# Features by relu and an exponential in place in PSUM, output low parts on GpSimd, P's low part in two halves

## The chip, the cores and the metric

The kernel runs on one core of one Trainium2 chip. The metric is device time in microseconds (us) of one execution. The core has five engines, each with its own instruction queue, in order: TensorE (PE, matmuls; PEld are its weight loads), VectorE (DVE), ScalarE (ACT), GpSimd (POOL) and SyncE (SP, which issues the DMAs here). SBUF is the working memory, PSUM the memory that matmuls write. In this kernel POOL works on SBUF only; DVE and ACT also read PSUM.

## The reference

Two layers, each of an attention with a compressive memory and of a gated MLP, with residuals:

```
x = x + A(layernorm(x)); x = x + B(layernorm(x))        # twice, S = 2048, D = 640

A: q, k, v = x@wq, x@wk, x@wv in 32 heads of 20, 4 segments of 512 rows; M = z = 0
   for each segment s:
       p    = softmax(qs ks^T / sqrt(20) + causal mask)
       phi(t) = t + 1 if t > 0 else exp(t)
       a_mem = (phi(qs) M) / (phi(qs) z + 1e-6)
       o    = g * a_mem + (1 - g) * (p vs)               # g = sigmoid(beta), by head
       M, z = M + phi(ks)^T vs, z + sum(phi(ks))
   return concat(o) @ wo
B: z = gelu(x@w_in); z1, z2 = halves; (w_sp @ layernorm(z2) + b_sp) * z1 @ w_out
```

All of it is in float32. The kernel gets there with float16 matmuls: a float32 value is split into a high part (its float16 rounding) and a low part (what is left, in float16), and a product takes three matmuls, high x high, high x low, low x high. Making a low part takes one operation that subtracts the high part from the value.

phi can be written without a branch as max(t, 0) + min(exp(t), 1). Both kernels use that form.

## The kernel before, in words

Each layer is three stages: attention (`phase1a`, class `Attention`), the output projection with the first MLP matmul (`phase1b`), and the spatial matmul with the last one (`phase2`). The change is in the attention, and in a few constants that the prologue makes.

**Attention by slots.** 64 pairs of heads (16 in each of 4 segments) are worked off at three slots each, 192 slots a layer; `run` (L912) writes their order out by hand. In slot t, for pair n = t // 3:

- `scores` (L793): PE forms a third of the transposed scores of pair n (tile `es`, one PSUM buffer) and a third of the untransposed scores of pair n + 2 (tile `mp`, one buffer), with the masks (L818, L790). ACT turns `es` into P by an exponential (L827). DVE takes row maxima of `mp` (L834) into `mx`; at a pair's last third it splits them into `mhs` (L838, L839, eight elements a row each).
- `pvs` (L865): PE multiplies P's high and low parts (PH, PL) with the values (L877), head h of pair n - 1 or so, three slots after they are made.
- `maxes` (L853): PE transposes `mhs` (`mtp`, L858), ACT copies it (L860), two DMAs on SP (L863) write it into two rows of the pair's q tile in `qk`, so that the scores come with their maxima subtracted.
- `cast` (L841): ACT rounds a head's P to float16 (PH, L849), POOL subtracts (PL, L850; 128 x 1280). PH and PL have two buffers each. For the last TAIL = 4 pairs of a layer, head 1's subtraction goes to DVE.
- `combine` (L881): DVE scales PV's sums (L888 to L893), POOL adds the halves and the memory's part (L894, L896) into `ot`; when a unit's heads are complete, `out` is posted two slots later: high part on ACT (L904), low part on DVE (L905), two DMAs on SP into `o_d` (L908).

**Dense work in between.** The rest of each slot on PE is filled with pieces of the next projections, by times planned in `run` (`plan`, `timed`, `until`): `value` (v of a row tile), `project` (wo for finished rows) and `unit` (L653), which forms q and then k of 128 of the 640 columns, each as 15 matmuls (L668) into a PSUM tile of tag "dn" (two buffers, shared by q, k, v and the projection). When such a tile is complete, `out` (L675) posts what follows for the next slots:

- one slot later `parts`: high part on ACT (L684), exp on ACT into the SBUF tile `e` (L687), low part on DVE (L688), and the store into DRAM (`stack`); exp only where a feature is needed, which is 15 of 20 q tiles and 15 of 20 k tiles a layer (60 tiles in both layers);
- another slot later `features`: DVE clips e at 1 and scales it (L694, from SBUF to SBUF), DVE adds max(q, 0) from PSUM (L696) and writes `phq` or `phk`; that frees the PSUM tile;
- for k another slot later `keys`: phi's high part on ACT (L704), low part on DVE (L705), and a transposing DMA for the memory's update.

Everything lives in scaled units; `rq` and `rk` turn a PSUM value back into the true q or k, `gq` and `gk` bring the clipped exponential into PSUM's units, `sig` scales phi(k) to float16's range, `epsd` is the reference's 1e-6 in these units.

**Who orders what.** Only PE's order is the one written out (`ENGINES`, L512). For DVE, ACT, POOL and SP the framework's scheduler chooses the order when the kernel is built, by program order and its own estimate of times, and sets the semaphores: an operation waits for what writes its input and for what still reads its output's place, and two engines do not use a PSUM tile at the same time.

Of the kernel before, what the change touches and what calls it, by code (L numbers as in the profile page):

```python
# [8 lines left out]
F32 = mybir.dt.float32  # L9
# [110 lines left out]
def prologue(g, ctx, wv, wq, wk, wo, w_in, w_out):  # L120

    nc, tc = g.nc, g.tc
    wp = ctx.enter_context(tc.tile_pool(name="wqkv", bufs=1))
    g.w = {}
    g.wo = Weight(g, "o", 3, wo, 0, D)
    g.wi = [Weight(g, "i0", 4, w_in, 0, FH), Weight(g, "i1", 5, w_in, FH, FH)]
    g.wu = Weight(g, "u", 6, w_out, 0, D)
    with tc.tile_pool(name="wpro", bufs=1, side="right", reuse_waits="tile") as p, \
            tc.tile_pool(name="wpp", bufs=1, space=PSUM, reuse_waits="tile") as pp:
        am = p.tile([128, 4, KD], F32, name="wamk")  # L130
        st = {}
        for i, (nm, dram) in enumerate((("v", wv), ("q", wq), ("k", wk))):
            st[nm] = p.tile([128, KD, D], F32, name="wst" + nm)
            for k in range(KD):
                nc.sync.dma_start(st[nm][:, k, :], dram[k * 128:(k + 1) * 128, :])
        for i, nm in enumerate("vqk"):
            with tc.high_priority(offset=HP if nm == "v" else 0):
                for k in range(KD):
                    nc.vector.tensor_reduce(am[:, i, k:k + 1], st[nm][:, k], AX.X, ALU.max, apply_absolute_value=True)
                nc.vector.tensor_reduce(g.wam[:, i:i + 1], am[:, i], AX.X, ALU.max)  # L140
                pow2_scales(g, p, pp, "wsc", g.wam, i, 1)
            h = wp.tile([128, KD, D], F16, name=f"w{nm}h")
            l = wp.tile([128, KD, D], F16, name=f"w{nm}l")
            for k in range(KD):
                if nm == "v":
                    split_scaled(g, h[:, k], l[:, k], st[nm][:, k], i)
                    continue
                w = st[nm][:, k]
                nc.scalar.activation(h[:, k], w, AF.Identity, scale=g.iv[:, i:i + 1])
                nc.scalar.activation(w, w, AF.Identity, scale=g.iv[:, i:i + 1])  # L150
                nc.gpsimd.tensor_tensor(l[:, k], w, h[:, k], ALU.subtract)
            g.w[nm] = (h, l)

    pq, pk = g.pw[:, 1:2], g.pw[:, 2:3]
    s = lambda n: g.sc[:, n:n + 1]
    g.esc, g.rq, g.rk, g.gq, g.gk, g.sig, g.epsd, g.yw, g.zi, g.pofs = s(0), s(1), s(2), s(3), s(4), s(5), s(6), s(7), (s(8), s(9)), s(10)
    nc.vector.tensor_scalar(g.esc, pq, pk, SCALE / 16, ALU.mult, ALU.mult)
    nc.vector.reciprocal(g.pofs, g.esc)
    nc.vector.tensor_scalar(g.pofs, g.pofs, LNPS / MS, None, ALU.mult)

    ph = g.qrow16
    nc.vector.tensor_copy(ph, g.pofs)
    nc.vector.tensor_tensor(g.qrow, g.pofs, ph, ALU.subtract)
    nc.vector.tensor_tensor(g.qrow, g.qrow, g.keep[:, 1:2], ALU.mult)
    nc.vector.scalar_tensor_tensor(g.qrow, g.keep[:, 0:1], ph, g.qrow, ALU.mult, ALU.add)
    nc.vector.tensor_scalar(g.rq, pq, 2.0 ** -24, None, ALU.mult)
    nc.vector.tensor_scalar(g.rk, pk, 2.0 ** -24, None, ALU.mult)
    nc.vector.tensor_scalar(g.gq, g.iv[:, 1:2], XS, None, ALU.mult)
    nc.vector.tensor_scalar(g.gk, g.iv[:, 2:3], XS, None, ALU.mult)
    nc.vector.tensor_scalar(g.sig, pk, 1.0, 2.0 ** -20, ALU.min, ALU.mult)  # L170
    nc.vector.tensor_scalar(g.epsd, g.gq, g.gk, None, ALU.mult)
    nc.vector.tensor_scalar(g.epsd, g.epsd, g.sig, 1e-6, ALU.mult, ALU.mult)


def other_scales(g, stage, pool, psum, tag):
# [288 lines left out]
def attn_consts(g, cp, beta):  # L464
    nc, tc = g.nc, g.tc

    g.eye = cp.tile([128, 64], F16, name="eye")
    g.step = {nm: cp.tile([128, 192], F16, name="step" + nm) for nm in "qk"}  # L470
    with tc.tile_pool(name="tmp", bufs=1) as tp, tc.tile_pool(name="acp", bufs=1, space=PSUM) as pp:
        f = tp.tile([128, 192], F32, name="fmask")
        for t, n, b, sg, op in ((g.eye, 64, 0, 1, ALU.not_equal), (g.step["q"], 192, -64, 1, ALU.is_ge), (g.step["k"], 192, 64, -1, ALU.is_ge)):
            nc.vector.memset(f, 0.0)
            for h in range(2):
                v = f[64 * h:64 * h + 64, :n]
                nc.gpsimd.affine_select(v, v, [[sg, n]], op, BIG if op is ALU.not_equal else -BIG, base=b, channel_multiplier=-sg)
            nc.vector.tensor_copy(t, f[:, :n])

        g.gate = cp.tile([128, H], F32, name="gate")  # L480
        g.iomg = cp.tile([128, H], F32, name="iomg")
        nc.sync.dma_start(g.gate, beta.rearrange("(o h) -> o h", o=1).to_broadcast((128, H)))
        nc.scalar.activation(g.iomg, g.gate, AF.Exp)
        nc.vector.tensor_scalar(g.iomg, g.iomg, 1.0, None, ALU.add)
        nc.scalar.activation(g.gate, g.gate, AF.Exp, scale=-1.0)
        nc.vector.tensor_scalar(g.gate, g.gate, 1.0, None, ALU.add)


        row = tp.tile([1, 3, 128], F32, name="mrow")
        nc.vector.memset(row, 0.0)  # L490
        for h in range(2):
            nc.vector.memset(row[:, 0, 64 * h + 62:64 * h + 63], 1.0)
            nc.vector.memset(row[:, 1, 64 * h + 63:64 * h + 64], 1.0)
            nc.vector.memset(row[:, 2, 64 * h + 60:64 * h + 64], MS)
        g.keep = cp.tile([128, 3], F32, name="keep")
        g.qrow = cp.tile([128, 1], F32, name="qrow")
        g.qrow16 = cp.tile([128, 1], F16, name="qrow16")
        kp = pp.tile([128, 4], F32, name="kp")
        for i in range(3):
            nc.tensor.matmul(kp[:, i:i + 1], row[:, i, :], g.ident[0:1, 0:1], start=True, stop=True)  # L500
        nc.vector.tensor_copy(g.keep, kp[:, 0:3])

    g.bmask = cp.tile([128, NU, 8], F32, name="bmask")
    nc.gpsimd.memset(g.bmask, 1.0)
    for m in range(NU):
        n, b = len(TH[m]), 128 * m - DH * TH[m][0]
        v = g.bmask[:, m, :n]
        nc.gpsimd.affine_select(v, v, [[-DH, n]], ALU.is_ge, 0.0, base=b, channel_multiplier=1)
        nc.gpsimd.affine_select(v, v, [[DH, n]], ALU.is_ge, 0.0, base=DH - 1 - b, channel_multiplier=-1)
# [5 lines left out]
class Attention:  # L515
# [159 lines left out]
    def out(self, nm, s, m, ps):  # L675

        g, nc = self.g, self.nc
        q = nm == "q"
        ph = []

        def parts():
            feature = s > 0 if q else s < NSEG - 1
            hl = self.u2.tile([128, 2, L], F16, tag="hl", name=f"{nm}hl")
            nc.scalar.mul(hl[:, 0], ps, QS)  # L684
            if feature:
                e = self.u2.tile([128, L], F32, tag="tmp", name="eq")
                nc.scalar.activation(e, ps, AF.Exp, scale=g.rq if q else g.rk)  # L687
            nc.vector.scalar_tensor_tensor(hl[:, 1], ps, QS, hl[:, 0], ALU.mult, ALU.subtract)  # L688
            self.stack(nm, s, m, hl)
            if feature:  # L690
                self.post(1, lambda: features(e))

        def features(e):
            nc.vector.tensor_scalar(e, e, 1.0, g.gq if q else g.gk, ALU.min, ALU.mult)  # L694
            ph.append((self.u4 if q else self.u1).tile([128, L], F32, tag=f"ph{nm}", name=f"ph{nm}"))
            nc.vector.scalar_tensor_tensor(ph[0], ps, 0.0, e, ALU.max, ALU.add)  # L696
            if q:
                self.phq[m] = ph[0]
            else:
                self.post(1, keys)  # L700

        def keys():
            hl = self.u2.tile([128, 2, L], F16, tag="hl", name="phl")
            nc.scalar.mul(hl[:, 0], ph[0], g.sig)  # L704
            nc.vector.scalar_tensor_tensor(hl[:, 1], ph[0], g.sig, hl[:, 0], ALU.mult, ALU.subtract)  # L705
            self.pk = self.u1.tile([128, 2, 4, 128], F16, tag="pk", name="pk")
            nc.sync.dma_start(self.pk.rearrange("p i t c -> p (i t) c"), hl.rearrange("p i c -> p (i c)"), transpose=True)

# [132 lines left out]
    def cast(self, n, h):  # L841
# [5 lines left out]
        PH = self.pl2.tile([128, 1280], F16, tag="PH", name="PH")  # L847
        PL = self.pl2.tile([128, 1280], F16, tag="PL", name="PL")
        nc.scalar.copy(PH, P[:, h])  # L849
        (nc.gpsimd if h == 0 or n < self.N - self.TAIL else nc.vector).tensor_tensor(PL, P[:, h], PH, ALU.subtract)  # L850
        self.P[n, h] = (PH, PL)

    def maxes(self, n):  # L853
# [27 lines left out]
    def combine(self, n, s, m, h0):  # L881
# [18 lines left out]
        def out():  # L900
            nh = len(UH[m])
            hl = self.e2.tile([128, 2, D], F16, tag="xh", name="ohl")[:, :, :4 * nh * DH].rearrange("p i (t h d) -> p i t h d", t=4, d=DH)
            oh, ol = hl[:, 0], hl[:, 1]
            nc.scalar.mul(oh, ot[:, :, :nh, :], 8.0)  # L904
            nc.vector.scalar_tensor_tensor(ol, ot[:, :, :nh, :], 8.0, oh, ALU.mult, ALU.subtract)  # L905
            c = slice(UH[m][0] * DH, (UH[m][0] + nh) * DH)
            for i, o in enumerate((oh, ol)):
                nc.sync.dma_start(self.o_d[s][:, i, c].rearrange("(t p) c -> p t c", p=128), o.rearrange("p t h d -> p t (h d)"))  # L908
# [205 lines left out]
```

## Time and profile before

| | us |
|---|---|
| time, median of 3 runs (lowest to highest) | 2518.58 (2512.72 to 2520.02) |
| profiled execution: its time | 2522.18 |
| profiled execution: span from first to last instruction | 2520.5 |
| es matmuls, first to last start (layer 0 begins, layer 1 ends) | 115.7 to 1926.7 |

The mean granted TensorE clock of the profiled execution is 0.955. A row of the view by lines reads: line, engine, operation, tile written <- tiles read, shapes out<-in, x count | busy us, mean ns of one | idle us of the engine ahead of them, and who ended it. A row of the waits reads: engine and line that waited <- what ended the wait: us in total, times, longest. A row of the view by stretch reads: start:end, length, then busy us (and number of instructions) of PE, PEld, DVE, ACT and POOL, then the granted clock, the DMA engines' share and GB/s. A row of a single line's view gives shortest/median/longest ns. In the timeline a row is start, us, engine, line, and in brackets the idle time ahead of it. SPq is SP's instruction queue.

### The profile page before, as it was taken

Reading aid. Unit: us, or ns where it says so; the run is one execution under the profiler, and the core shown is the slowest. Engines: PE = TensorE matmul, PEld = TensorE weight load, DVE = VectorE, ACT = ScalarE, POOL = GpSimd, SP = SyncE. Lnnn points to the kernel's source line nnn. Section 1 sums busy time; section 2 is a strip of 40 time slices with the busy share of each in tenths; the row PEclk is TensorE's granted clock in tenths of the full one; section 3 lists DMA queues with packets and bytes.
Section 4 is the critical chain, followed back from the end, with each engine's and each line's share of the span. In section 5 each row is a group of like instructions: output and inputs, shape, how many; then the busy total and the mean of one; then the engine's idle time right before and its main releaser. Section 6 shows DMA issues by size and latency. Waiting matters only on the chain. (4 is left out here: it accounts for less than half of the span.)

```text
span 2520.5 us, 52420 instructions
## 1 busy us (share of the span) xinstructions
PE 2237.1 (89%) x21706; PEld 1332.5 (53%) x21706; DVE 1555.7 (62%) x2925; ACT 1137.3 (45%) x1388; POOL 945.9 (38%) x715
## 2 busy tenths in 40 slices
PE   3678787798889998999987889889898999999998
PEld 2345454465555554555554546546565555555554
DVE  6678977887854444544435787788886545444431
ACT  4267766686642322211113777667675322111110
POOL 7156666687731100000032777767775100000000
PEclk9889999899999999999998999989999999999999
DMA  4733644423563378766643344342346336776752
GB/s 141 204 95 102 165 109 104 107 69 107 130 173 93 93 206 223 186 157 169 148 103 89 81 115 105 93 107 75 96 115 163 99 98 161 175 185 167 154 139 59
DMA packets 504575, 325.11 MB, mean 129 GB/s; under 512 B 410576, under 2 KB 445520, under 8 KB 499216
## 3 DMA queue, kind: packets, MB, share of 16 engines
q1 hardware_dynamic: 504336, 321.77, 50.1%
q8 instruction: 169, 2.77, 0.5%
q14 instruction: 70, 0.57, 0.1%
HBM read 148.26 MB, written 85.34 MB: 93 GB/s over the span
## 5 line engine op out<-in xcount | busy, mean ns | idle before, releaser
L850 POOL TENSOR_TENSOR PL<-P,PH 128x1280 f16<-128x1280 f32 x248 | 652.1, 2632 | 285.8 <-ACT PH L849 237.7
L834 DVE TENSOR_REDUCE mx<-mp 128x2 f32<-128x1024 f32 (+3 forms) x512 | 408.3, 818 | 114.6 <-PE mp L790 113.2
L381 PE MATMUL gp<-zh,wt 128*128 128x432 f16 x2048 | 466.4, 348 | 11.3 <-DMA wt<-wn 11.3
L827 ACT ACTIVATE P<-es,sc 128x1024 f32<-128x1024 f32 (+1 forms) x384 | 371.3, 967 | 206.2 <-PE mp L790 163.6
L381 PEld LDWEIGHTS <-wt 128*128 128x128 f16 x3072 | 301.7, 98 | 273.1 <-DMA wt<-wn 12.6
L849 ACT CAST PH<-P 128x1280 f16<-128x1280 f32 x256 | 321.1, 1255 | 9.2 <-PE pv L877 1.8
L300 PEld LDWEIGHTS <-th 128*128 128x128 f16 x1920 | 188.2, 98 | 170.7 <-issue 6.6
L381 PE MATMUL gp<-zl,wt 128*128 128x432 f16 x1024 | 272.4, 348 | 0.0
L396 POOL MEMSET un<- 128x64 f16 x32 | 4.8, 151 | 682.2 <-DMA ut<-un 629.5
L818 PEld LDWEIGHTS <-qk 64*128 64x128 f16 (+1 forms) x2048 | 83.3, 96 | 289.3 <-issue 225.0
L212 POOL TENSOR_TENSOR lnrs<-lnve,mhalf 128x1 f32<-128x1 f32 x96 | 58.4, 616 | 449.1 <-DVE lnve L211 432.3
L358 DVE TENSOR_REDUCE am<-wr 128x1 f32<-128x2048 f32 x32 | 73.1, 2286 | 207.2 <-DMA wr<-in_B_w_sp_dram 207.2
L384 ACT ACTIVATE u<-gp,bsp,un 128x864 f32<-128x864 f32 x32 | 34.2, 1068 | 362.8 <-PE gp L381 362.8
L818 PE MATMUL es<-qk 64*128 64x512 f16 (+3 forms) x1024 | 143.0, 314 | 58.3 <-ACT P L827 48.9
L818 PE MATMUL mp<-qk 60*128 60x512 f16 (+3 forms) x1024 | 141.8, 312 | 54.9 <-DVE mx L834 54.3
L608 PE MATMUL vps<-wvh,xt 128*128 128x320 f16 x640 | 163.5, 325 | 25.3 <-DMA xt<-xnhl 8.4
L410 PE MATMUL cyp<-wuh,ut 128*128 128x320 f16 (+1 forms) x896 | 165.6, 302 | 9.1 <-DMA ut<-un 9.1
L877 PE MATMUL pv<-vs,PH 128*128 128x41 f16 x2560 | 168.0, 183 | 0.0
L410 PEld LDWEIGHTS <-ut 128*128 128x128 f16 (+1 forms) x1344 | 132.3, 99 | 65.7 <-DMA ut<-un 10.2
L877 PE MATMUL pv<-vs,PL 128*128 128x41 f16 x2560 | 164.4, 181 | 1.6 <-POOL PL L850 1.6
L368 ACT ACTIVATE wn<-wr,ivw 128x1024 f16<-128x1024 f32 x64 | 71.9, 1144 | 181.4 <-DVE ivw L363 94.4
L300 PE MATMUL zp<-wi1h,th 128*128 128x432 f16 x640 | 149.1, 348 | 4.1 <-DMA th<-xnhl 3.5
(188 smaller groups left out, 4346.3 us busy)
## 6 DMA issues: line engine op xcount, KB each, us to landing
wr<-in_B_w_sp_dram SPq DMA_DIRECT2D x32, 1024.0 KB
qk<-st SPq DMA_DIRECT2D x256, 120.0 KB
z<-z SPq DMA_DIRECT2D x32, 432.0 KB
cz<-z SPq DMA_DIRECT2D x32, 432.0 KB
xt<-in_A_x_dram SPq DMA_DIRECT2D x32, 320.0 KB
st<-qhl SPq DMA_DIRECT2D x40, 256.0 KB
st<-khl SPq DMA_DIRECT2D x40, 256.0 KB
x<-x SPq DMA_DIRECT2D x32, 320.0 KB
```

Source lines behind the costliest of these rows:

```text
L300: nc.tensor.matmul(zp[:, n, :FHH], a[:, k, :], b[:, k, c:c + FHH], start=(k == 0 and j == 0), stop=(k == KD - 1 and j == 2))
L358: nc.vector.tensor_reduce(am, wr, AX.X, ALU.max, apply_absolute_value=True)
L368: nc.scalar.activation(hl[:, 0], wr[:, c], AF.Identity, scale=ivw)
L381: nc.tensor.matmul(gp[:, n, :FHH], wt[:, k // 8, a, k % 8, :], b[:, k, n * FHH:(n + 1) * FHH], start=(k == 0 and j == 0), stop=(k == NT - ...
L410: nc.tensor.matmul(yp[:, n, :320], a[:kn[k], k, :], b[:kn[k], k, n * 320:(n + 1) * 320], start=(k == 0 and j == 0), stop=(k == KO - 1 and ...
L608: nc.tensor.matmul(ps, a[:, k, c], b[:, k, n * 320:(n + 1) * 320], start=(i == 0), stop=(i == 14))
L818: nc.tensor.matmul(out[:, h, o:o + w], a[r, ac], b[r, bc], start=o == 0, stop=False, skip_group_check=True)
L827: nc.scalar.activation(P[:, :, 512 * c:512 * c + ew], es[:, :, :ew], AF.Exp, scale=g.esc)
L834: nc.vector.tensor_reduce(self.mx[m][:, :, i], mp[:, :, o:o + w], AX.X, ALU.max)
L849: nc.scalar.copy(PH, P[:, h])
L850: (nc.gpsimd if h == 0 or n < self.N - self.TAIL else nc.vector).tensor_tensor(PL, P[:, h], PH, ALU.subtract)
L877: nc.tensor.matmul(pv[:, i, h, :], x[:, c:c + 128], v[:, j, h0 + h, :], start=(j == 0 and x is PH), stop=(j == i and x is PL), skip_group_ ...
```

## The change

1. *Features.* `parts` computes relu(r * q) on ACT into SBUF, where it computed the exponential. `features` computes exp(r * q) on ACT in place, over q's or k's own PSUM tile, and one DVE operation, min(PSUM, 1) + relu, makes phi (for q into `phq`, for k over the relu's tile). The clip-and-scale operation on DVE (L694) is gone, and so is the tile `phk`. phi is now in true units, so the constants `gq` and `gk` go, and `sig` and `epsd` change.
2. *Outputs.* The gates' denominators carry a factor 1/8, so that `ot` comes out 8 times larger and `out` need not multiply. The high part is a copy on ACT; the low part is a subtraction on POOL where it was an operation on DVE.
3. *P's low part.* The subtraction of 128 x 1280 is two of 128 x 640, on the engine that had it.

```diff
-    nc.vector.tensor_scalar(g.gq, g.iv[:, 1:2], XS, None, ALU.mult)
-    nc.vector.tensor_scalar(g.gk, g.iv[:, 2:3], XS, None, ALU.mult)
-    nc.vector.tensor_scalar(g.sig, pk, 1.0, 2.0 ** -20, ALU.min, ALU.mult)
-    nc.vector.tensor_scalar(g.epsd, g.gq, g.gk, None, ALU.mult)
-    nc.vector.tensor_scalar(g.epsd, g.epsd, g.sig, 1e-6, ALU.mult, ALU.mult)
+    nc.vector.tensor_scalar(g.sig, g.iv[:, 2:3], 1.0 / WTOP, 1.0, ALU.mult, ALU.min)
+    nc.vector.tensor_scalar(g.sig, g.sig, 16.0, None, ALU.mult)
+    nc.vector.tensor_scalar(g.epsd, g.sig, 1e-6, None, ALU.mult)
...
-        nc.vector.tensor_scalar(g.iomg, g.iomg, 1.0, None, ALU.add)
+        nc.vector.tensor_scalar(g.iomg, g.iomg, 1.0, 0.125, ALU.add, ALU.mult)
...
-        nc.vector.tensor_scalar(g.gate, g.gate, 1.0, None, ALU.add)
+        nc.vector.tensor_scalar(g.gate, g.gate, 1.0, 0.125, ALU.add, ALU.mult)
...
             if feature:
-                e = self.u2.tile([128, L], F32, tag="tmp", name="eq")
-                nc.scalar.activation(e, ps, AF.Exp, scale=g.rq if q else g.rk)
+                r = self.u2.tile([128, L], F32, tag="tmp", name="relu")
+                nc.scalar.activation(r, ps, AF.Relu, scale=g.rq if q else g.rk)
             nc.vector.scalar_tensor_tensor(hl[:, 1], ps, QS, hl[:, 0], ALU.mult, ALU.subtract)
             self.stack(nm, s, m, hl)
             if feature:
-                self.post(1, lambda: features(e))
-
-        def features(e):
-            nc.vector.tensor_scalar(e, e, 1.0, g.gq if q else g.gk, ALU.min, ALU.mult)
-            ph.append((self.u4 if q else self.u1).tile([128, L], F32, tag=f"ph{nm}", name=f"ph{nm}"))
-            nc.vector.scalar_tensor_tensor(ph[0], ps, 0.0, e, ALU.max, ALU.add)
+                self.post(1, lambda: features(r))
+
+        def features(r):
+            nc.scalar.activation(ps, ps, AF.Exp, scale=g.rq if q else g.rk)
             if q:
-                self.phq[m] = ph[0]
+                self.phq[m] = self.u4.tile([128, L], F32, tag="phq", name="phq")
+                nc.vector.scalar_tensor_tensor(self.phq[m], ps, 1.0, r, ALU.min, ALU.add)
             else:
-                self.post(1, keys)
-
-        def keys():
+                nc.vector.scalar_tensor_tensor(r, ps, 1.0, r, ALU.min, ALU.add)
+                self.post(1, lambda: keys(r))
+
+        def keys(ph):
             hl = self.u2.tile([128, 2, L], F16, tag="hl", name="phl")
-            nc.scalar.mul(hl[:, 0], ph[0], g.sig)
-            nc.vector.scalar_tensor_tensor(hl[:, 1], ph[0], g.sig, hl[:, 0], ALU.mult, ALU.subtract)
+            nc.scalar.mul(hl[:, 0], ph, g.sig)
+            nc.vector.scalar_tensor_tensor(hl[:, 1], ph, g.sig, hl[:, 0], ALU.mult, ALU.subtract)
...
         nc.scalar.copy(PH, P[:, h])
-        (nc.gpsimd if h == 0 or n < self.N - self.TAIL else nc.vector).tensor_tensor(PL, P[:, h], PH, ALU.subtract)
+        for c in (slice(0, 640), slice(640, 1280)):
+            (nc.gpsimd if h == 0 or n < self.N - self.TAIL else nc.vector).tensor_tensor(PL[:, c], P[:, h, c], PH[:, c], ALU.subtract)
...
-            nc.scalar.mul(oh, ot[:, :, :nh, :], 8.0)
-            nc.vector.scalar_tensor_tensor(ol, ot[:, :, :nh, :], 8.0, oh, ALU.mult, ALU.subtract)
+            nc.scalar.copy(oh, ot[:, :, :nh, :])
+            nc.gpsimd.tensor_tensor(ol, ot[:, :, :nh, :], oh, ALU.subtract)
```

More of the change, by code (lines that the diff above doesn't have):

```diff
@@ L678, in out @@
         q = nm == "q"
-        ph = []
         def parts():
```

## The prediction, made before the change was timed

> **What bounds the kernel now.** I began with the page: TensorE (PE) is busy most of the time, no other engine is near its limit over the span.
>
> ```profile
> span 2520.5 us, 52420 instructions
> ...
> PE 2237.1 (89%) x21706; PEld 1332.5 (53%) x21706; DVE 1555.7 (62%) x2925; ACT 1137.3 (45%) x1388; POOL 945.9 (38%) x715
> ```
>
> The change touches the attention stage only, so the next view is busy time by stretch, over the attention of layer 0 and of layer 1, with their sum:
>
> ```profile
> 115.00:745.00 630.00, 526.02 (x7389) 328.83 (x7388) 500.68 (x916) 429.95 (x537) 412.61 (x266) 0.92 0.44 114
> 1395.00:1935.00 540.00, 464.23 (x6942) 297.59 (x6941) 437.12 (x822) 390.41 (x488) 396.52 (x257) 0.95 0.42 106
> sum 1170.00, PE 990.24 PEld 626.42 DVE 937.80 ACT 820.35 POOL 809.13; mean PE 495.12 PEld 313.21 DVE 468.90 ACT 410.18 POOL 404.56
> ```
>
> Here DVE is nearly as full as PE: 938 of 1170 us (80%), ACT 70%, POOL 69%. PE stands idle for 1170 - 990 = 180 us; that is all the change can win. The waits of PE alone, for the same two stretches, say for whom:
>
> ```profile
> PE mtp L858 <- DVE mhs L839: 34.3, 13, 7.5
> PE mp L818 <- DVE mx L834: 27.4, 25, 3.9
> PE es L818 <- ACT P L827: 25.9, 35, 2.2
> ...
> PE pv L877 <- POOL PL L850: 0.8, 1, 0.8
> ```
>
> ```profile
> PE es L818 <- ACT P L827: 22.0, 34, 2.7
> PE mtp L858 <- DVE mhs L839: 19.5, 8, 5.2
> PE mp L818 <- DVE mx L834: 19.4, 18, 4.2
> ...
> PE pv L877 <- POOL PL L850: 0.8, 1, 0.8
> ```
>
> For DVE: 53.8 us (mtp for mhs) and 46.8 us (mp for mx), 100.6 together. For ACT's P: 47.9 us. For POOL: 1.6 us. DVE is what PE waits for most.
>
> Why is DVE late? The views of single lines give shortest, median and longest duration:
>
> ```profile
> L850 POOL TENSOR_TENSOR PL<-P,PH x248: 2598/2617/3184, 124.4 to 1929.2; 128x1280 f16<-128x1280 f32 x124
> L838 DVE TENSOR_SCALAR mhs<-mx x128: 154/172/2603, 108.9 to 1916.7; 128x8 f16<-128x8 f32 x128
> L839 DVE SCALAR_TENSOR_TENSOR mhs<-mx,mhs x128: 111/167/2625, 109.5 to 1917.2; 128x8 f16<-128x8 f32 x128
> L694 DVE TENSOR_SCALAR eq<-eq,sc x60: 471/1022/2499, 75.9 to 1849.6; 128x512 f32<-128x512 f32 x60
> L591 DVE TENSOR_SCALAR xt<-xt,lnmv,lnrs x32: 592/613/2901, 19.7 to 1685.4; 128x640 f32<-128x640 f32 x32
> L905 DVE SCALAR_TENSOR_TENSOR ohl<-oat,ohl x40: 595/657/3248, 162.8 to 1937.7; 128x480 f16<-128x480 f32 x32, 128x640 f16<-128x640 f32 x8
> L705 DVE SCALAR_TENSOR_TENSOR phl<-phk,sc,phl x30: 734/751/2995, 80.6 to 1708.1; 128x512 f16<-128x512 f32 x30
> ```
>
> An operation on eight elements that takes 0.17 us at the median and 2.6 us at worst was held up, and the longest extra is one PL on POOL (2.617 us). One stretch of the timeline shows it, and what it does to PE:
>
> ```profile
> 1815.62 5.62 POOL L850 TENSOR_TENSOR PL<-P,PH 128x1280 f16<-128x1280 f32 x2 [0.67 <-ACT PH L849]
> 1816.13 2.58 DVE L838 TENSOR_SCALAR mhs<-mx 128x8 f16<-128x8 f32 x1
> 1818.74 2.52 DVE L839 SCALAR_TENSOR_TENSOR mhs<-mx,mhs 128x8 f16<-128x8 f32 x1
> 1821.32 0.29 PE L858 MATMUL mtp<-ident,mhs 128*128 128x128 f16 x1 [5.24 <-DVE mhs L839]
> ```
>
> Two PLs run, the first mhs ends about when the first PL ends, the second about when the second does, and PE stood for 5.24 us. So a DVE operation that reads only SBUF, or two SBUF operands, waits out the POOL instruction under way, and gets in between two of them.
>
> **The change part by part.** Counts and mean durations, over the whole run:
>
> ```profile
> L850 POOL TENSOR_TENSOR PL<-P,PH 128x1280 f16<-128x1280 f32 x248 | 652.1, 2632 | 285.8 <-ACT PH L849 237.7 <-PE mp L790 22.9 <-ACT mr L860 17.4
> L694 DVE TENSOR_SCALAR eq<-eq,sc 128x512 f32<-128x512 f32 x60 | 61.5, 1024 | 0.0
> L838 DVE TENSOR_SCALAR mhs<-mx 128x8 f16<-128x8 f32 x128 | 53.0, 414 | 2.7
> L839 DVE SCALAR_TENSOR_TENSOR mhs<-mx,mhs 128x8 f16<-128x8 f32 x128 | 44.8, 350 | 3.4
> L591 DVE TENSOR_SCALAR xt<-xt,lnmv,lnrs 128x640 f32<-128x640 f32 x32 | 43.9, 1375 | 6.5 <-POOL lnrs L212 6.3
> L905 DVE SCALAR_TENSOR_TENSOR ohl<-oat,ohl 128x480 f16<-128x480 f32 (+1 forms) x40 | 40.1, 1002 | 3.2 <-ACT ohl L904 3.1
> L705 DVE SCALAR_TENSOR_TENSOR phl<-phk,sc,phl 128x512 f16<-128x512 f32 x30 | 32.5, 1082 | 3.4 <-ACT phl L704 3.4
> L696 DVE SCALAR_TENSOR_TENSOR phk<-kps,eq 128x512 f32<-128x512 f32 x30 | 20.6, 685 | 0.0
> L687 ACT ACTIVATE eq<-kps,sc 128x512 f32<-128x512 f32 x30 | 20.3, 677 | 0.0
> L827 ACT ACTIVATE P<-es,sc 128x1024 f32<-128x1024 f32 (+1 forms) x384 | 371.3, 967 | 206.2 <-PE mp L790 163.6 <-PE es L790 33.2 <-POOL lnrs L212 7.3
> L684 ACT ACTIVATE khl<-kps 128x512 f16<-128x512 f32 x40 | 23.6, 590 | 30.9 <-PE kps L668 30.2 <-DVE wap L188 0.7
> L151 POOL TENSOR_TENSOR wql<-wstq,wqh 128x640 f16<-128x640 f32 x5 | 6.9, 1394 | 0.0
> L894 POOL TENSOR_TENSOR oat<-ab 128x160 f32<-128x160 f32 x128 | 77.0, 602 | 72.4 <-DVE ab L893 67.7 <-PE mp L790 2.9 <-ACT mr L860 0.9
> ```
>
> *Features.* L694 goes: 60 x 1.024 = 61.5 us of DVE, 33 us of it waiting for POOL. L696 stays as one operation with a PSUM and an SBUF operand, 0.69 us as now (above: L705's 1.08, if it were held up like an operation with two SBUF operands; I take 0.69, the same operand places). On ACT the relu takes the place of the exponential in the same slot with the same operands, 0.68 for 0.68, nothing (the trace has no relu; L684's 0.59 is the lower end). The in-place exponential is new work: 60 x 0.677 = 40.8 us (floor: L684's 0.59, 35 us). It adds a wait: the exponential overwrites a bank that DVE's subtraction (L688) must have read. Behind it in ACT's queue stand the slot's PH casts and the next P, and PE's es waits for that P (L827, one in each of 384 slots). PE had to wait for it in 35 + 34 = 69 slots (18%). At that share 7 us of the 40.8 come through, at worst all 41; I take 12, nearer the low end, since ACT idles 1170 - 820 = 350 us here and L688 belongs to the slot before. The PSUM tile is freed after 0.68 + 0.69 us in place of 1.02 + 0.69, across one more engine, and the next value or projection tile that needs the bank is formed no earlier: nothing, unless ACT runs late, which is rival 1.
>
> [...]
>
> *Outputs' low parts.* L905 goes: 40.1 us of DVE. POOL gets 32 of 480 elements and 8 of 640. From L894 (160 elements, 0.60) and L151 (640, 1.39) a line gives 1.11 at 480: 32 x 1.11 + 8 x 1.39 = 47 us. POOL takes them in its own order, behind PLs, and SP's queue, which writes each output by two DMAs (L908), stands until they are made; queued behind are the loads of qk and the row maxima (L863):
>
> ```profile
> SPq L908 <- DVE ohl L905: 16.2, 15, 4.8
> ```
>
> ```profile
> PEld L818 <- DMA qk<-mr: 11.5, 10, 4.3
> ```
>
> SP waits 16 us for L905 today. If each of 40 came a half PL later, 40 x 1.3 = 52 us more; PE waits only 11.5 us for the maxima, which have most of three slots to arrive. I take +3 us (0 to 52). [...]
>
> *PL in halves.* A half is L151's operation: 2 x 1.39 = 2.79 for 2.63, so 248 x 0.16 = 39 us more POOL. With 47 that is 86 us, POOL goes from 69% to 77%. PV waited 1.6 us in all for PL, and the half that PV reads first comes 1.2 us sooner; I take +3 us (0 to 86). The 8 PLs that DVE makes at a layer's end cost it about 1 us in all. The gain is for DVE: one hold-up is at most 1.39 us. What is held up beyond the median today: L838 (414 - 172) x 128 = 31.0, L839 23.4, L591 24.4, L705 9.9, together 89 us. A lone operation would keep 0.53 of its wait; of a pair the second often meets the other half, so I take 0.6 kept, 35 us less.
>
> DVE's load thus falls by 61.5 + 40.1 + 35 = 137 us, from 80% to 68%, nearly all of it in these two stretches.
>
> *What of it reaches PE.* The mtp wait (53.8 us) is as long as the extra of the mhs pair that it waits for (31.0 + 23.4 = 54.4). At 0.6 it is 32; L694 and L905 no longer stand ahead of the pair, I take 10 more, so 22 stay and 32 are won (bounds 0 and 54). The mp wait (46.8 us) comes from DVE's backlog. DVE's free share grows from 20% to 32%, a backlog drains 1.6 times as fast: 29 stay, 18 are won (from 7, in proportion to the load, to 47; a loss is excluded as far as DVE goes, which is given no new operation). Next late is P on ACT, which is the +12.
>
> Prologue and gates lose two 0.15-us operations: nothing.
>
> Sum: -32 - 18 + 12 + 3 + 3 = -32 us. The profiled execution took 2522.18 us (1.7 us of it around the span), so 2490; the median of the runs, 2518.58, lies 3.6 lower, so I forecast 2486 us. About 0.3% (7.6 us) is what can be told from no change. With the bounds that I believe possible (-75, nearly all that PE waits for DVE without the ACT term growing, to -10) the forecast's own range is 2444 to 2509.
>
> **Rivals.**
>
> 1. *ACT becomes the bound (slower).* The exponential stands at the head of ACT's queue until DVE's L688 is through, and P behind it. Price: 0.68 plus half a hold-up (0.70), 60 times, 83 us if PE waits for all of it; with 50 won and 6 lost that is +39, or 2558 by the median. It decides once more than 44/83 (53%) comes through. For it: es waits for P already, 47.9 us. Against it: ACT's 350 us of idle time. 14%.
> 2. *Hidden anyway (no change).* PE, freed from DVE, meets P that was just behind: half of the 50 comes back, and the ACT, POOL and SP terms are doubled by another order of the engines' queues: -25 + 24 + 6 + 6 = +11 at the worst, and nothing if they only grow by 40%; I count 2511 to 2526 as this. For it: the waits for P (47.9 us) are as large as those for mx. Against it: the waits for mhs are few and long, 53.8 us in 21, and es is not what PE comes to next after an mtp. 12%.
> 3. *POOL becomes the bound.* All 86 us come in front of PV: -50 + 12 + 86 = +48, 2567. It decides from 38 us. Against it: 1.6 us of waits today, and POOL has 23% left. 4%.
> 4. *Relu and exponential reload ACT's function table.* The trace has such a load ahead of a first exponential:
>
> ```profile
> L687 ACT ACT_TABLE_LOAD  x1: 1283/1283/1283, 1337.0 to 1337.0; - x1
> ```
>
> Two per feature are 120 x 1.283 = 154 us on ACT; if all of it reaches PE, -32 + 154 = +122, or 2641. The trace has no relu to judge by. [...] 2%.
>
> **How the numbers follow.** The forecast has 68% and all of its own range is faster by over 0.3%; rival 2 is no change; rivals 1, 3 and 4, 20% together, are slower. So faster 0.68, same 0.12, slower 0.20. The range 2440 to 2530 takes in the forecast, rival 2 and the lower half of rival 1 (2526 to 2558); it leaves out the other half (7%), rivals 3 and 4 (6%) and a tail below (5%).
>
> **What would show it.** Right: longest L838 and L839 near 1.4 us; DVE some 130 us less; mtp's wait near 22 and mp's near 29; no table load inside attention. Wrong: es waiting for P over 80 us, with an exponential ahead of it (rival 1), pv waiting for PL over 20 us (3). If mhs is still held up for 2.6 us, both halves run before DVE gets in, and my middle term is gone.

## The result, and the profile after

| | before | changed |
|---|---|---|
| time, median of 4 runs each, us (lowest to highest) | 2515.65 (2511.48 to 2520.02) | 2447.94 (2442.78 to 2450.51) |
| ratio of changed to before, 95% interval | | 0.9728 (0.9702 to 0.9754) |
| profiled execution, us | 2522.18 | 2449.39 |

The change wins 68 us (2.7%). The forecast was 2486 us, 32 us won; the way was right and the gain is a little over twice as large. In two kernels further down (features and halves, thirds) one execution took several hundred us or more beyond the others, and their medians are of the other three.

The page of the changed kernel, its span and the engines' busy time:

```profile
span 2447.7 us, 52666 instructions
...
PE 2211.2 (90%) x21706; PEld 1324.1 (54%) x21706; DVE 1451.7 (59%) x2831; ACT 1167.5 (48%) x1448; POOL 1018.8 (42%) x1003
```

PE issues the same 21706 matmuls, yet is busy 26 us less (2237.1 before). Busy time by stretch shows where. For this comparison each layer's attention goes from its first `es` matmul to its last; before, that is

```profile
115.70:712.10 596.40, 495.63 (x7141) 310.29 (x7141) 480.25 (x878) 416.62 (x523) 404.45 (x258) 0.92 0.43 111
1368.00:1927.10 559.10, 479.54 (x7137) 305.10 (x7137) 450.18 (x842) 405.72 (x508) 402.48 (x258) 0.95 0.41 104
sum 1155.50, PE 975.18 PEld 615.39 DVE 930.43 ACT 822.34 POOL 806.94; mean PE 487.59 PEld 307.70 DVE 465.21 ACT 411.17 POOL 403.47
```

and in the changed kernel

```profile
111.80:664.60 552.80, 476.94 (x7139) 303.90 (x7139) 424.76 (x836) 429.88 (x551) 439.74 (x400) 0.96 0.46 120
1319.30:1851.60 532.30, 470.81 (x7138) 301.79 (x7138) 403.09 (x798) 420.27 (x537) 437.44 (x400) 0.97 0.43 109
sum 1085.10, PE 947.75 PEld 605.69 DVE 827.85 ACT 850.15 POOL 877.18; mean PE 473.88 PEld 302.84 DVE 413.93 ACT 425.08 POOL 438.59
```

Nearly all of the gain is there: 1155.5 - 1085.1 = 70 us, of 73 between the two profiled spans. Of it PE's idle time gives 180.3 - 137.3 = 43 us, and PE's busy time 975.2 - 947.8 = 27 us, for the same matmuls. The column behind POOL's points at a reason: the mean granted clock rose from 0.92 and 0.95 to 0.96 and 0.97. By the clock's record PE had half the clock for 154 us of the two stretches before, and for 82 us of them now.

PE's waits in the two stretches, changed kernel:

```profile
PE es L814 <- ACT P L823: 26.4, 38, 1.9
PE mp L814 <- DVE mx L830: 17.2, 20, 1.9
PE mtp L855 <- DVE mhs L835: 10.8, 6, 3.4
```

```profile
PE es L814 <- ACT P L823: 24.3, 37, 2.3
PE mp L814 <- DVE mx L830: 14.4, 16, 2.1
PE mtp L855 <- DVE mhs L835: 5.8, 5, 1.7
```

mtp's wait for mhs fell to 16.6 us and mp's for mx to 31.6; ACT's P is now what PE waits for most. The operations that could be held up, and what holds them up:

```profile
L834 DVE TENSOR_SCALAR mhs<-mx x128: 157/282/1437, 105.0 to 1839.3; 128x8 f16<-128x8 f32 x128
L835 DVE SCALAR_TENSOR_TENSOR mhs<-mx,mhs x128: 148/168/1362, 105.2 to 1840.0; 128x8 f16<-128x8 f32 x128
L847 POOL TENSOR_TENSOR PL<-P,PH x496: 1389/1402/1984, 123.5 to 1855.1; 128x640 f16<-128x640 f32 x166
```

The longest hold-up is one half of PL, as forecast; the median of the first operation has gone up, from 0.172 to 0.282 us: they are held up more often (30 of 128 take over 0.5 us, 23 before). The new work, by lines:

```profile
L690 ACT ACTIVATE qps<-qps,sc 128x512 f32<-128x512 f32 x30 | 19.5, 649 | 6.8 <-DVE qhl L684 6.7
L690 ACT ACTIVATE kps<-kps,sc 128x512 f32<-128x512 f32 x30 | 19.3, 642 | 5.6 <-DVE khl L684 5.6
L690 ACT ACT_TABLE_LOAD x1 | 1.3, 1283 | 0.0
L902 POOL TENSOR_TENSOR ohl<-oat,ohl 128x480 f16<-128x480 f32 (+1 forms) x40 | 46.4, 1160 | 22.1 <-ACT ohl L901 21.4 <-PE pv L874 0.7
```

**Why the clock.** The trace records the granted clock in stretches of 3.41 us or whole multiples of it, at 1 or at one half. Four such stretches of the kernel before, around one wait of mtp for mhs:

```profile
629.49:632.91 3.42, 3.42 (x47) 1.70 (x42) 2.80 (x5) 3.30 (x5) 3.42 (x4) 1.00 0.21 72
632.91:636.32 3.41, 1.38 (x33) 0.94 (x32) 3.41 (x5) 2.97 (x3) 2.88 (x2) 1.00 0.38 122
636.32:639.73 3.41, 3.34 (x20) 1.34 (x22) 1.92 (x5) 0.25 (x1) 1.34 (x2) 0.50 0.01 1
639.73:643.15 3.42, 3.02 (x60) 1.80 (x56) 2.74 (x5) 2.82 (x4) 2.18 (x2) 1.00 0.19 48
```

In the second PE works 1.38 of 3.41 us and stands for the rest; in the third it is busy, with half the clock. So this wait of 2 us was paid once as idle time and again as matmuls that took longer: the 128x512 matmul of L668 takes 0.38 us at the median from 609.1 to 636.0 us, at the full clock, and 0.63 from 602.19 to 609.02, at half of it. Counted over the whole trace of the kernel before, in stretches of 3.41 us at the full clock: where PE was idle for over 60% the next stretch had half the clock (29 of 29), where it was idle for less than 35% the next never had (0 of 595), and between the two 12 of 38 had. The theory from here on is "long waits": only waits long enough to empty most of a stretch cost that much here, and what counts on DVE is the longest lateness, not the load. The rivals: "load", the gain follows DVE's busy time; "chance clock", PE's busy time has nothing to do with the waits.

### The profile page after: what moved, and what is told of

Same layout as the page of the kernel before. It is cut to its first block, busy times and chain, and to the rows that moved or that the text cites. A ratio compares the mean times of both kernels' runs of the same rounds, so it can differ in the third digit from the quotient of the medians.

```text
span 2447.7 us, 52666 instructions
## 1 busy us (share of the span) xinstructions
PE 2211.2 (90%) x21706; PEld 1324.1 (54%) x21706; DVE 1451.7 (59%) x2831; ACT 1167.5 (48%) x1448; POOL 1018.8 (42%) x1003
## 5 line engine op out<-in xcount | busy, mean ns | idle before, releaser
L847 POOL TENSOR_TENSOR PL<-P,PH 128x640 f16<-128x640 f32 x496 | 690.8, 1416 | 195.1 <-ACT PH L845 183.3
L394 POOL MEMSET un<- 128x64 f16 x32 | 4.9, 152 | 685.8 <-DMA ut<-un 632.7
L382 ACT ACTIVATE u<-gp,bsp,un 128x864 f32<-128x864 f32 x32 | 34.2, 1069 | 358.7 <-PE gp L379 358.6
L814 PE MATMUL es<-qk 64*128 64x512 f16 (+3 forms) x1024 | 141.0, 308 | 59.5 <-ACT P L823 50.7
```

The source lines that it names most:

```text
L814: nc.tensor.matmul(out[:, h, o:o + w], a[r, ac], b[r, bc], start=o == 0, stop=False, skip_group_check=True)
```

## The experiments

Each kernel was timed in three rounds beside the kernel before on the same chip. For each the table gives the time, what it won against the kernel before there, and, for the two stretches of attention together, PE's busy and idle time, DVE's busy time and the three waits of PE, in us.

| kernel | time | won | PE busy | PE idle | DVE busy | mtp, mhs | mp, mx | es, P |
|---|---|---|---|---|---|---|---|---|
| before | 2515.7 | | 975.2 | 180.3 | 930.4 | 54.4 | 49.7 | 48.9 |
| features alone | 2471.9 | 46.7 | 957.9 | 157.7 | 854.1 | 24.4 | 33.1 | 57.4 |
| outputs alone | 2487.8 | 30.8 | 961.7 | 160.5 | 896.6 | 39.6 | 46.1 | 46.0 |
| halves alone | 2472.9 | 45.7 | 953.7 | 150.1 | 895.7 | 40.0 | 32.1 | 48.6 |
| features and outputs | 2470.4 | 48.2 | 951.3 | 159.3 | 835.1 | 23.8 | 34.2 | 57.1 |
| outputs and halves | 2469.5 | 52.4 | 956.5 | 149.6 | 889.4 | 37.8 | 36.0 | 39.8 |
| features and halves | 2452.6 | 65.6 | 945.2 | 143.1 | 839.0 | 19.2 | 33.0 | 54.7 |
| all (the change) | 2447.9 | 67.7 | 947.8 | 137.3 | 827.9 | 16.6 | 31.6 | 50.7 |

### The parts alone, and the change less one part

Each part is its hunks of the diff above, put into the kernel before or taken out of the changed one; nothing else changes.

Features alone. 

> The kernel before with the features alone changed (relu and in-place exponential; P's low part whole, outputs' low parts on VectorE). Theory 'long waits': PE loses time to the few long waits for VectorE, once as idle time and once more because each wait of about 2 us and more is followed by a stretch at half the granted clock; so what counts is how long the longest hold-ups are. The whole PL of 2.6 us is still there, so mhs is still held up by 2.6 us at worst: waits of mtp 35 to 50 us, PE busy in the attention falls by 5 to 10 of the 27 us, time -20 to -30 us against before. Rival 'load': the gain follows VectorE's busy time, 70 us won for 103 us less: with 62 us less here -38 to -45 us. Rival 'chance clock': PE's busy time differs between runs whatever the change: no relation of PE busy to the waits over these kernels.

Outputs alone. 

> The kernel before with the outputs' low parts alone on GpSimd (and the factor 8 in the gates). 40 us less on VectorE, 46 us more on GpSimd. Long waits: some of the mhs waits had a held-up L905 ahead of them, the hold-ups of mhs by PL stay: -5 to -15 us. Load: -27 us. A third possibility, SyncE's queue standing for the later low parts: 0 to +10 us, with PE waiting over 20 us for qk<-mr.

Halves alone. 

> The kernel before with P's low part alone in two halves. VectorE has the same work; each hold-up is 1.4 us at most in place of 2.6. Long waits: mtp waits fall from 54 to 25 us or less, the granted clock rises from 0.955 to 0.96 or more, PE busy falls by 10 us or more, time -25 to -40 us although the sum of the hold-ups falls by less than a third. Load: VectorE busy falls by 20 to 30 us: -14 to -20 us.

The change with PL whole. 

> The changed kernel with P's low part whole again (features and outputs as changed). Long waits: mtp waits come back to 30 us or more, clock 0.96, time 25 to 35 us above the changed kernel. Load: VectorE busy 20 us more than in the changed kernel: 10 to 15 us above it.

The ratios to the kernel before are 0.9805 (0.9784 to 0.9826), 0.9866 (0.9840 to 0.9892), 0.9807 (0.9784 to 0.9830) and 0.9792 (0.9769 to 0.9816). Halves alone speak against load: 35 us less DVE time and 46 us won, as much as the features win with 76 us less. The hold-ups of mhs hardly shrank in sum (54 us to 50), but they did in length, and those over 1.5 us went from 17 to none; in the kernel with halves alone the first of the pair reads

```profile
L838 DVE TENSOR_SCALAR mhs<-mx x128: 153/172/1398, 107.0 to 1862.8; 128x8 f16<-128x8 f32 x128
```

I was too low on the features (20 to 30 expected, and mtp at 35 to 50; load's figure was nearer): with L694 out of DVE's queue mhs was also late less often. PL whole costs 20 of the 68 us, between both expectations. Over nearly all rows PE's busy time moves with its idle time, which speaks against chance; half-clock time in the two stretches goes from 154 us to 111 with the features, 127 with the outputs, 90 with the halves and 82 with all.

The change less the features. 

> Outputs' low parts on GpSimd and halves, with the features as before: what the features bring on top of the other two. If the three parts added up (47 + 31 + 46 = 124 us when alone) the features would bring 47 and this kernel would be at 2495. Long waits: the parts work on the same waits, so on top of the others each brings less: 2460 to 2472, and the waits of es for P stay at 46 to 50 us, with no cost of the exponential to be seen. If ACT's new exponential costs PE the 12 us that were forecast, es waits for P by 8 us or more less here than with the features.

The change less the outputs. 

> The changed kernel with the outputs' low parts on VectorE again: features and halves. The outputs brought 31 us alone and 1.5 us on top of the features. If they bring as little on top of both others, this kernel is within 8 us of the changed one; if they are worth their 31 us again, at 2479.

0.9804 (0.9778 to 0.9829) and 0.9746 (0.9713 to 0.9779). The parts win 47 + 31 + 46 = 124 us alone and 68 together: they work on the same waits. On top of the other two, features are worth about 15 us, halves 20, outputs 2, which the intervals of the two ratios don't tell from nothing. The ACT term is seen here: with outputs and halves in both, es waits 39.8 us for P without the features and 50.7 with them, 11 us more; features alone raise it by 8.5. Why outputs on GpSimd bring 31 us alone and 1.5 on top of the features was not settled.

### Extra work on VectorE, in short and in long pieces

First as an operation that depends on nothing (shown is the long form; the short one has it at every pair, with 4 in place of 18):

```diff
+                if m % 4 == 0:
+                    scr = self.pl2.tile([128, 18], F32, tag="scr", name="scr")
+                    nc.vector.tensor_reduce(scr, g.ident.unsqueeze(1).to_broadcast((128, 18, 128)), AX.X, ALU.max)
                 mh = self.mhs[m % 2][:, :16].rearrange("p (h i t) -> p h i t", h=2, i=2)
```

> The changed kernel with an extra operation on VectorE at each of the 128 pairs, ahead of mhs: a maximum over 512 constants whose result nobody reads (work added, about 0.6 us each, some 75 us in all, never held up by GpSimd). Long waits: each is too short to make PE wait for long; the sum of PE's waits over 1.5 us stays under 55 us (43 in the changed kernel), half-clock time under 100 us, time 5 to 20 us above the changed kernel. Load: VectorE's busy time is back to 905 us in the attention, between the changed kernel (829 us, 2448) and the one before (930 us, 2519): 45 to 55 us above the changed kernel.

> The same work in long pieces: at every fourth pair (32 times) a maximum over 2304 constants, about 2.5 us each, some 78 us in all. Long waits: PE waits over 1.5 us at most of the 32, their sum rises by 40 us or more, half-clock time by 35 us or more, PE busy by 12 us or more; time 45 to 80 us above the changed kernel, and at least 25 us above the short pieces. Load: as the short pieces, 45 to 55 us above the changed kernel.

2472.0 us (0.9808, 0.9783 to 0.9834) and 2504.3 us (0.9931, 0.9909 to 0.9954). Both told nothing of the two theories: as the operation needs nothing, the build's scheduler put all of them ahead of the two layers' attention. DVE's busy time inside is 833 and 834 us, close to the changed kernel's 828, while the stretch ahead of layer 0's first `es` grew from 112 to 121 and 137 us. Then with an operand that holds them in place, the pair's own maxima (short: every pair, 64 in place of 288):

```diff
+                if m % 4 == 0:
+                    scr = self.pl2.tile([128, 288], F32, tag="scr", name="scr")
+                    nc.vector.tensor_reduce(scr, mx.rearrange("p h i -> p (h i)").unsqueeze(1).to_broadcast((128, 288, 8)), AX.X, ALU.max)
```

> The short pieces again, now made to stay in their place: the extra maximum reads the pair's mx (512 elements, result unread), so that VectorE cannot do it ahead of the attention; about 0.67 us at each of 128 pairs, 85 us in all, right ahead of mhs. Long waits: PE's waits over 1.5 us rise from 43 to under 60 us, half-clock time from 82 to under 105 us, time 8 to 25 us above the changed kernel. Load: VectorE is back at 912 us in the attention: 50 us or more above the changed kernel.

> The same work in 32 long pieces of about 2.5 us (2304 elements, from mx too), right ahead of mhs at every fourth pair. Long waits: PE's waits over 1.5 us rise by 30 us or more, half-clock time by 30 us or more, PE busy in the attention by 10 us or more with the same matmuls; time 35 to 80 us above the changed kernel, and at least 20 us above the short pieces. Load: as the short pieces, within 10 us of them. Chance clock: half-clock time does not follow the waits.

The extra work, short and long, by lines:

```profile
L835 DVE TENSOR_REDUCE scr<-mx 128x64 f32<-128x512 f32 x128 | 87.5, 683 | 3.1
```

```profile
L835 DVE TENSOR_REDUCE scr<-mx 128x288 f32<-128x2304 f32 x32 | 81.7, 2552 | 1.0
```

Short: 2484.2 us (ratio 0.9864, 0.9838 to 0.9891). Long: 2587.7 us (1.0272, 1.0242 to 1.0303), for 6 us less work: 104 us between them. Of the reductions themselves none was held up (the short ones took 0.66 to 0.69 us). The long pieces' attention:

```profile
118.10:730.90 612.80, 501.35 (x7141) 315.86 (x7141) 458.25 (x836) 431.85 (x550) 437.94 (x398) 0.91 0.40 104
1394.70:1979.20 584.50, 488.86 (x7138) 308.73 (x7138) 433.49 (x800) 423.20 (x534) 434.81 (x398) 0.93 0.38 97
sum 1197.30, PE 990.21 PEld 624.59 DVE 891.74 ACT 855.06 POOL 872.75; mean PE 495.11 PEld 312.30 DVE 445.87 ACT 427.53 POOL 436.38
```

Against the changed kernel the attention is 112 us longer, 70 of it idle and 42 in PE's busy time; with the short pieces (1100.6 us, PE busy 953.4) it is 15.5 us longer. Load falls here: the same work, seven times the price in the attention. I had put the long pieces at 35 to 80 us over the whole run; they cost 140, the short ones 36. Outside the attention both kernels lose alike, so this does not touch the 104 us between them: 4.6 and 6.3 us ahead of layer 0's first `es`, 17 and 19 us in the MLP stages. The traces suggest a reason for the latter: the changed kernel does the first two row tiles of each MLP's layer norm (L216) before the attention ends, at 632.7 and 636.5 us in layer 0, and the kernels with the extra work do them behind it, at 692.1 and 694.5 us in the short one. That this is what costs the 17 us was not tested.

### The same lateness, with PE kept at work

The long pieces stay, and at the same pairs PE gets 20 useless matmuls ahead of mtp:

```diff
-        tp = self.pm.tile([128, 512], F32, tag="ms", name="mtp")[:, :128]
+        tp = self.pm.tile([128, 512], F32, tag="ms", name="mtp")
+        for _ in range(20 if n % 4 == 0 else 0):
+            nc.tensor.matmul(tp[:, 128:320], g.ident16, g.step["k"], start=True, stop=True)
+        tp = tp[:, :128]
```

> The kernel with the long pieces in place (2588 us), and at the same 32 pairs 20 matmuls on TensorE whose result nobody reads, queued right ahead of mtp, so that PE works while mhs is late (work added). Theory 'long waits cost twice': PE's waits for mhs are partly filled, fewer stretches at half the clock follow; half-clock time falls from 202 to 140 us or less, and the kernel is 15 to 45 us faster than with the long pieces alone, although PE got 640 matmuls more. Rival 'only the wait counts': the fillers fit into waits of some 3 us or lengthen them a little: 0 to 15 us slower than 2588, half-clock time where it was.

```profile
115.90:708.50 592.60, 502.40 (x7438) 328.39 (x7438) 459.95 (x838) 431.73 (x549) 439.31 (x399) 0.96 0.42 108
1372.80:1947.60 574.80, 496.53 (x7437) 326.34 (x7437) 433.33 (x801) 422.37 (x534) 435.94 (x398) 0.97 0.39 99
...
```

```profile
L859 PE MATMUL mtp<-stepk,ident 128*128 128x192 f16 x640 | 59.6, 250 | 0.0
```

2550.5 us (ratio 1.0133, 1.0108 to 1.0157): 37 us faster than the long pieces alone, with 640 matmuls more. The clock is back at 0.96 and 0.97 (82 us at half the clock, 202 with the long pieces alone), and PE's busy time without the fillers is 502.4 + 496.5 - 59.6 = 939 us, 51 us less than with the long pieces. The lateness of VectorE is still there: on top of the 60 us of fillers PE waits 63 us for mhs, where it had waited 109. That is the second price of a wait, taken away by itself.

### Smaller pieces of PL

Only the slices change: four of 320, then three (432, 432, 416).

> The changed kernel with P's low part in four pieces of 320. A hold-up is 0.8 us at most; GpSimd gets some 256 x 0.3 = 80 us more work, to about 955 of 1085 us (88%). Long waits: mtp's wait falls from 17 to 10 us or less, time 3 to 12 us below the changed kernel as long as GpSimd keeps up. GpSimd as the bound: PE waits over 10 us for PL, or VectorE and ACT for GpSimd's other work, and the time is 5 to 40 us above.

2478.5 us (0.9842, 0.9812 to 0.9873), 24 us less won than with halves. Neither expectation says why; the timeline shows what was new:

```profile
546.00 1.55 POOL L847 TENSOR_TENSOR PL<-P,PH 128x320 f16<-128x320 f32 x2
546.68 7.36 DVE L834 TENSOR_SCALAR mhs<-mx 128x8 f16<-128x8 f32 x1
547.51 0.52 POOL L893 TENSOR_TENSOR oat<-oat,gm 128x160 f32<-128x160 f32 x1
547.99 6.03 POOL L847 TENSOR_TENSOR PL<-P,PH 128x320 f16<-128x320 f32 x8
554.08 0.17 DVE L835 SCALAR_TENSOR_TENSOR mhs<-mx,mhs 128x8 f16<-128x8 f32 x1
```

DVE did not get in between the pieces: its operation stood through eleven POOL instructions, for 7.36 us, until POOL ran out of work. Four more of the 128 took 4.1 to 5.0 us. A hold-up of one piece is no law.

> The changed kernel with P's low part in three pieces (432, 432, 416). In quarters (0.81 us each) mhs's first operation was held up through several pieces in a row, up to 7.4 us, in halves (1.40 us) never through more than one. If what lets VectorE in between two pieces depends on their length, thirds (about 1.0 us) lie between: hold-ups over 2 us now and then and 2450 to 2475; if it is only GpSimd's load, which thirds bring from 877 to about 905 us: no hold-up over 1.2 us and 2440 to 2452.

2455.2 us (0.9756, 0.9728 to 0.9784), 65.1 us won, 2.6 less than with halves, which the intervals don't tell apart. No hold-up over 1.37 us; the longest were under another POOL operation. POOL is at 911 us of 1091 here and at 947 of 1116 in quarters. Whether length or load lets DVE in stays open.

### The exponential in SBUF, and mhs's high part on ScalarE

```diff
+                e = self.u1.tile([128, L], F32, tag="e", name="eq")
...
-            nc.scalar.activation(ps, ps, AF.Exp, scale=g.rq if q else g.rk)
+            nc.scalar.activation(e, ps, AF.Exp, scale=g.rq if q else g.rk)
...
-                nc.vector.scalar_tensor_tensor(self.phq[m], ps, 1.0, r, ALU.min, ALU.add)
+                nc.vector.scalar_tensor_tensor(self.phq[m], e, 1.0, r, ALU.min, ALU.add)
```

> The changed kernel with the exponential written to an SBUF tile of its own in place of the PSUM tile, so that VectorE's one operation has two SBUF operands and no PSUM operand; ACT's work is the same (0.68 in place of 0.65 us). Those 60 operations can now be held up by GpSimd: 0.69 becomes about 0.95 on the mean and 2.1 at worst, some 15 us more VectorE. Long waits: 5 to 15 us above the changed kernel. If the place of the exponential does not matter: within 4 us.

2459.7 us (0.9757, 0.9731 to 0.9784): 9 us less won than by the change, as expected, though the two intervals still overlap. The operation on q takes 1.14 us on the mean and that on k 0.98, against 0.68 each with a PSUM operand. By these times the place of the exponential is worth about that.

```diff
-                nc.vector.tensor_scalar(mh[:, :, 0], mx, -1.0 / MS, None, ALU.mult)
+                nc.scalar.mul(mh[:, :, 0], mx, -1.0 / MS)
```

> The changed kernel with mhs's high part made by ScalarE in place of VectorE (128 operations of eight elements), so that only one of the pair can be held up by GpSimd. Long waits: the mtp waits fall from 17 to 10 us or less and the time by 3 to 12 us, unless the new handover from VectorE to ScalarE and back puts mhs behind ScalarE's P and PH (1 to 1.3 us each): then mtp waits rise over 25 us and the time by 5 to 25 us.

2522.0 us (1.0006, 0.9990 to 1.0022): 69 us worse than the change, far over the 25 I had allowed, and not by ScalarE's queue alone:

```profile
300.51 1.26 ACT L845 CAST PH<-P 128x1280 f16<-128x1280 f32 x1 [0.21 <-PE pv L874]
301.68 0.20 ACT L834 ACTIVATE mhs<-mx 128x8 f16<-128x8 f32 x1
301.85 2.76 POOL L847 TENSOR_TENSOR PL<-P,PH 128x640 f16<-128x640 f32 x2 [3.34 <-ACT PH L845]
301.91 1.36 DVE L835 SCALAR_TENSOR_TENSOR mhs<-mx,mhs 128x8 f16<-128x8 f32 x1 [1.56 <-ACT mhs L834]
```

PH's end starts POOL's next piece, and mhs's high part right behind PH releases DVE's operation just after it. What was held up now and then (14 of 128 over 0.5 us) is held up three times in four (98): L835's median is 1.353 us there, 0.168 in the changed kernel, while its longest, 1.367, is the changed kernel's 1.362. So the longest lateness is not all: PE waits for mhs 96 times, about 1 us each, 95 us in all. Its idle time, some 198 us, is above that of the kernel before (a few matmuls are missing in this trace, so it is a little less), yet half-clock time is 104 us against 154: these waits of 1 us cost mostly their length, and far less of the clock than those of 2 us and more did. No kernel tried here beats the change.

## Why the prediction fell short

**What bounds the kernel: right as to DVE, wrong as to the limit.** The largest waits of PE were for DVE, and they are what fell. But PE's idle time, 180 us, was not "all the change can win": its busy time could fall too.

**"What of it reaches PE": the step that failed.** The forecast took as the price of a wait the time that PE stood. It put mtp's wait at 22 us and mp's at 29; measured are 16.6 and 31.6. Idle time fell by 43 us where the whole sum was 32. But the sum had no term for the matmuls themselves: 27 us of PE's busy time went too, because fewer half-clock stretches follow. Of the 38 us by which the sum fell short in the attention, this missing term is 27, and idle time the other 11. The filled kernel shows that this loss is caused by the waits and can be had or not had by itself. The rows quoted for the bound carried it already, the granted clock of 0.92 and 0.95; I read past the column.

**"I take 0.6 kept": wrong, and without harm.** Of the mhs pair's 54.4 us beyond the median, (382 - 172) x 128 + (349 - 167) x 128 = 50 us remain (382 and 349 ns are the changed kernel's means): 0.92. DVE's busy time fell by 103 us in the attention, not 137. mtp's wait fell all the same, since it is long hold-ups that make PE wait, not their sum; that the two sums were alike before (53.8 and 54.4) was no ground to scale one by the other. The split was off too: the forecast gave 22 us of this term to the halves and 10 to L694 and L905 leaving the queue; alone, the halves took 14 us off mtp's wait and the features 30.

**mp's wait: the number right by luck.** The 18 us came from DVE's free share growing from 20% to 32%. It grew to 24% (827.9 of 1085.1 us busy), which by the same rule would win 8 us; 18 were won. With halves alone DVE is as full as before, 895.7 of 1103.8 us (81%), and the mp wait fell from 49.7 to 32.1 all the same. So it does not follow DVE's share; that it follows the length of the hold-ups, as mtp's does, fits the rows but was not shown for mp by itself.

**The ACT term (+12): right in size for P, hidden in the sum.** The features alone raise es's wait for P by 8.5 us, on top of the other parts by 11; shorter lateness of DVE takes as much off again, so before and after differ by 1.8 us. Two waits that the sum put at nothing grew by 6 us each: for ACT's copy mr (11.0 to 16.8 us) and for the PSUM tile that the feature operation on k frees (1.0 to 6.6). These two, P's 1.8, and mtp and mp with 56 us less account for the 43 us of idle time within a microsecond or two.

**POOL and SP (+3 each): nothing.** pv waits 1.5 us for PL in all; es waits 6.3 us for the maxima's DMA (7.3 before).

**The rivals.** ACT as the bound: es waits 50.7 us, not over 80. Hidden anyway: no. POOL: no; with 877 of 1085 us busy it made PV wait 1.5 us. Table reloads: the one load at L690 (1.28 us) is the one that was there at L687.

## What to carry to other kernels

When another engine makes PE wait, read the granted clock of that stretch with the waits, and price the waits by both the idle time and the slower matmuls behind them: here the change won 43 us of the one and 27 of the other. Look at how long a small operation on the path takes at worst, and how often, rather than at the engine's load: some 85 us of extra work cost 15 us of attention in short pieces and 112 in long ones, and the kernel with a hold-up of 1.4 us at three pairs in four lost 69 us. Parts that shorten the same waits do not add up, so measure them together.

## What the runs showed of the hardware

- The VectorE operations L838, L839, L694, L591, L705 and L905 of the kernel before, all on SBUF alone, waited out a PL under way on GpSimd: begun with over 0.1 us of it left, 103 times, they ended behind it 102 times. With a whole PL (2.62 us at the median) mhs's two took 2.60 and 2.63 us at most, against medians of 0.17; with halves (1.40), in the changed kernel, 1.44 and 1.36. The operation that makes phi, with a PSUM operand, did not wait (0.67 us at least and 0.69 at most, in both kernels).
- The prediction put that too widely, for every operation that reads only SBUF: in the kernel before, the reciprocal at L889 took 0.18 to 0.21 us all 128 times (0.19 at 240.34 us, 0.26 us into a PL of 2.62), and the `tensor_scalar` on one element a row at L211 0.09 to 0.16 us all 96 times (0.14 at 1645.52, 0.45 us into another); in the kernel with the short pieces in place the extra reductions of mx took 0.66 to 0.69 us.
- In quarters, mhs's `tensor_scalar` was passed over by a run of short instructions (7.36 us behind eleven, most of 0.8 us); that befell it alone, while the operation with two SBUF operands behind it took 1.33 us at most there.
- The granted clock of the kernel before halved after each stretch of 3.41 us at the full clock in which PE was idle for over 60% (29 of 29, 632.91 to 639.73 us above among them), and after none with less than 35% (0 of 595).
- ScalarE's exponential of 128x512 from PSUM to PSUM took 0.65 us on the mean in the changed kernel (L690), from PSUM to SBUF 0.68 in the kernel before (L687).
